# When the next piece of x is asked for: one transform slot earlier, from batch 2 on

## The chip, the cores and the metric

The kernel runs on one core of one Trainium2 chip. The metric is the device time of one execution in microseconds (us). Beside it one execution was profiled; every start time below counts from the start of that profile's span.

## What is computed

The reference mixes eight sequences with a Fourier transform and feeds the result to a mixture of experts (MoE). Cut to what matters:

```python
X = np.fft.rfft(x, axis=1)                  # x: 8 x 2496 x 256, float32
Yr = Xr @ w_r - Xi @ w_i + b_r
Yi = Xr @ w_i + Xi @ w_r + b_i
Yr, Yi = soft_threshold(Yr, 0.01), soft_threshold(Yi, 0.01)
x = np.fft.irfft(Yr + 1j * Yi, n=2496, axis=1)      # 19968 rows of 256
expert = argmax(x @ w_gate)                 # 8 experts
# per expert: the 80 rows of the largest gate value (softmax of x @ w_gate)
out[rows] = gate * (relu(x[rows] @ w1[e]) @ w2[e])  # all other rows are zero
```

## The kernel before

**Stages.** 2496 is 39 x 64, and the transform is done in two steps with a trip through HBM between them. Stage A (`stageA`, L283) multiplies a piece of x by a 39-point table, three blocks of 39 rows at a time on 117 partitions. Its result `zs`, split into a high and a low float16 half (`stageAz`, L303, on ACT and DVE), is stored to the HBM buffer `zd` (L319). `loadZ` (L329) reads it back turned round, stage B (L341) does the 64-point step, stage C (L394) the two weight products and the threshold, stage D (L485) turns the result and adds the gate columns, and stage HB (L524) does the first part of the way back and stores it to the HBM buffer `hd` (L539, L547). Once per batch stage E stores gate parts to `gd` (L675, L676) and reads them back as `gr` (L679) for a small product on TensorE (L723). After the eight batches the kernel chooses the rows, gathers them, runs the experts and scatters the rows into an output that `zfill` (L255, store at L259) has filled with zeros in 56 stores, most of 384 KB.

**The loop.** The main loop (L1346) has 16 steps, two per batch (`ch` 0 in an even step, 1 in an odd one). A step writes down the instructions of stages C and B, of D and HB for the step before, and three calls of `doA`, the transform slots: L1416, L1435 and L1448, here S1, S2 and S3. One slot transforms half a piece of x of a batch that comes two batches later. Steps 0 and 1 have more slots (8 and 4), so that batches 1 and 2 are done by the end of step 1; from step 2 on, batch b takes the six slots of one even and one odd step.

**Pieces.** A batch of x is three pieces, here (b,0), (b,1) and (b,2). `loadX` (L265) fetches one with three DMAs of 39 rows each on SP's queue: 3 x 312 KB for the first two, 234 + 234 + 156 KB for the third (39 rows x 8, 6 or 4 columns x 256 x 4 bytes). It goes into one of three buffers `xt`. A piece is transformed in two slots, a first and a second half. One slot ahead of its use a half is split into two float16 parts `xs` (`halve`, L275): a copy on ACT (L280), then a subtraction on GpSimd (L281), both of which wait for the piece's DMAs. There are two buffers `xs`.

**Who asks for the next piece.** `preX` (L1277) asks for pieces until two are waiting in the list `xls`, which by then doesn't hold the piece that is being transformed. `doA` (L1282) calls it when the second half of a piece has been written down (L1292). The piece asked for goes into the buffer of the piece before the present one. While `hold` is set (the last but one slot of step 0) `preX` does nothing.

**What orders SP's queue.** The instructions of an engine are issued in one fixed order, which a scheduler makes out of the order in which the program writes them down: an instruction that is ready sooner may be placed ahead of older ones, except that tiles of one name get their buffers in the written order. `pin` (`keep_in_program_order`, L161) ties an instruction behind the one that was written down just before it on the same engine. The loads of x (L270) and the zero stores (L259) are pinned; the stores to `zd` and `hd` and the loads of `z` are not. Stores are written down late: `flush` (L154) writes those that are pending, and it is called inside the stages.

Of the kernel before, what the change touches and what calls it, by code (L numbers as in the profile page):

```python
# [132 lines left out]
def fourier_mix_then_moe(ctx, tc, x, w_r, w_i, b_r, b_i, wg, w1, w2, t1, t2, vq, v3, v0, v1f, vt, sg, cst, cb, out):  # L133
# [131 lines left out]
    def loadX(b, c, xt=None):  # L265
        if xt is None:
            xt = zaq.tile([117, 8, 256], F32, name="xt", bufs=3)
        xv = x[b].rearrange("(a n) d -> a n d", n=64)
        for s, n in spans(c):
            pin(nc.sync.dma_start(xt[39 * s:39 * s + 39, :n], xv[:, 22 * s + 8 * c:22 * s + 8 * c + n]))  # L270
        return xt
# [3 lines left out]
    def halve(b, q, xt):  # L275
        j0 = 4 * (q % 2)
        ng = min(4, 22 - 4 * q)
        K = 117 if q < 5 else 78
        xs = halves[b, q] = zaq.tile([117, 2, 4, 256], F16, name="xs", bufs=2)
        nc.scalar.activation(xs[:K, 0, :ng], xt[:K, j0:j0 + ng], AF.Copy)  # L280
        nc.gpsimd.tensor_tensor(xs[:K, 1, :ng], xt[:K, j0:j0 + ng], xs[:K, 0, :ng], op=ALU.subtract)  # L281

    def stageA(b, q, xt):  # L283
        j0 = 4 * (q % 2)
        ng = min(4, 22 - 4 * q)
        K = 117 if q < 5 else 78
        xv = xt[:K, j0:j0 + ng]
        pt = psum()
        if b:
            if (b, q) not in halves:  # L290
                halve(b, q, xt)
            xs = halves.pop((b, q))
        for j in range(ng // 2):
            if b:
                for i, (t, h) in enumerate(((0, 0), (0, 1), (1, 0))):
                    nc.tensor.matmul(pt[:K, 512 * j:512 * j + 512], t1s[:K, t, :K], xs[:K, h, 2 * j:2 * j + 2], start=(i == 0), stop=(i == 2))  # L296
                continue
            nc.tensor.matmul(pt[:K, 512 * j:512 * j + 512], t1f[:K, :K], xv[:, 2 * j:2 * j + 2], start=True, stop=True)
        stageAz(b, q, K, ng, pt)
# [977 lines left out]
    def preX():  # L1277
        while len(xls) < 2 and Xq and not hold:
            a = Xq.pop(0)
            xls.append((a, loadX(*a)))  # L1280

    def doA(n=1):  # L1282
        for _ in range(n):
            if not Aq:
                if not xls:
                    preX()
                if xls:
                    (b, c), xt = xls.pop(0)
                    Aq.extend([(b, 2 * c, xt), (b, 2 * c + 1, xt)])
            if Aq:  # L1290
                stageA(*Aq.pop(0))
            if not Aq:  # L1292
                preX()
            if Aq:
                halve(*Aq[0])
            elif xls:
                (b, c), xt = xls[0]
                halve(b, 2 * c, xt)
# [47 lines left out]
    for i in range(len(steps)):  # L1346
        b, ch = steps[i]
# [66 lines left out]
        if i > 0:  # L1414
            zfill()
        doC(0, 0); doB(); doA(); doHB(); doB()  # L1416
        doP({12: 0, 13: 0, 14: 0}.get(i, 1)); doW({12: 1, 13: 1, 14: 1}.get(i, 1))
        if pend3:
# [11 lines left out]
        if i == 0:  # L1430
            doA(3)
        doP({12: 0, 13: 1, 14: 0}.get(i, 1)); doW({12: 1, 13: 1, 14: 1}.get(i, 1))
        if i > 0:
            zfill()
        doC(1, 0); doB(); doD(); doA(); doHB(); doD()  # L1435
        doP({12: 3, 13: 0, 14: 2}.get(i, 1)); doW({12: 1, 13: 1, 14: 1}.get(i, 1))
        if prev:
# [172 lines left out]
```

## Time and profile before

| | |
|---|---|
| time, median of 3 runs | 648.32 us (645.98 to 655.67) |
| the profiled execution's own time | 649.41 us |
| its span (first to last instruction) | 647.2 us, 2.2 us less |
| TensorE matmul (PE) busy | 543.1 us, 84% of the span |
| VectorE (DVE), GpSimd (POOL), ScalarE (ACT) busy | 426.5, 384.2, 335.2 us |
| moved by DMA | 133.17 MB, 206 GB/s on the mean |

PE is TensorE with its matmuls, PEld its weight loads. A name with q (SPq) is an engine's sequencer, which waits and issues DMAs. "Idle before" is the time that an engine sat idle just before an instruction, and "<-" names what ended it. Such a releaser is inferred: where an engine is named that had long been done, or a DMA of another buffer, the wait ended with a DMA that landed at that time. "DMA share" is the mean busy share of the core's 16 DMA engines; it can come out a little over 1.

### The profile page before, as it was taken

The page shows a single profiled execution, that of the slowest core. Times are in us where ns is not written, and L with a number is a line of the kernel's source. Part 1 is how long each engine was busy: PE and PEld are TensorE (multiplying, and loading weights), DVE is VectorE, ACT ScalarE, POOL GpSimd, SP SyncE. Part 2 cuts the span into 40 slices and gives each one's busy share as a digit, 9 for nine tenths or more (in the row PEclk, how much of TensorE's full clock was granted, in tenths as well). Part 3 has the DMA queues.
Part 4 walks back from the last instruction along what each step waited for, and adds up shares of the span by engine and source line. Part 5 has one row for each costly group of instructions (what it writes and reads, how often), then busy time and mean ns, then how long its engine had stood idle before and what let it go on. Part 6 is the DMA issues. An engine that isn't in the chain of part 4 may idle for free. (4 is left out here: it accounts for less than half of the span.)

```text
span 647.2 us, 12925 instructions
## 1 busy us (share of the span) xinstructions
PE 543.1 (84%) x5002; PEld 395.7 (61%) x5003; DVE 426.5 (66%) x768; ACT 335.2 (52%) x483; POOL 384.2 (59%) x292
## 2 busy tenths in 40 slices
PE   6349779999789998998999889988799895967783
PEld 2136447667666776685776557756577674436673
DVE  3424425476557665775776796689999977955870
ACT  1325546566546575574666545654656727411561
POOL 2014757676836775675768457667863458455671
PEclk7778979999999999998999989989899868888887
DMA  7797879689679968987997896699745368457630
GB/s 175 247 221 178 229 177 284 194 248 207 194 205 292 225 180 218 271 235 197 270 214 221 210 283 182 186 261 276 170 139 164 83 216 262 122 158 267 219 121 29
DMA packets 96456, 133.17 MB, mean 206 GB/s; under 512 B 27038, under 2 KB 78253, under 8 KB 94517
## 3 DMA queue, kind: packets, MB, share of 16 engines
q1 hardware_dynamic: 88885, 114.64, 67.0%
q0 software_dynamic: 2128, 9.25, 4.2%
q10 hardware_dynamic: 5376, 8.39, 4.1%
q8 instruction: 41, 0.67, 0.4%
q14 instruction: 26, 0.21, 0.1%
HBM read 69.58 MB, written 62.67 MB: 204 GB/s over the span
## 5 line engine op out<-in xcount | busy, mean ns | idle before, releaser
L406 PE MATMUL ps<-XT,WM 128*128 128x288 f16 (+1 forms) x1536 | 224.2, 304 | 15.0 <-ACT XT L355 6.0
L406 PEld LDWEIGHTS <-WM 128*128 128x128 f16 x1536 | 152.3, 100 | 77.2 <-issue 18.4
L281 POOL TENSOR_TENSOR xs<-xt,xs 117x1024 f16<-117x1024 f32 (+1 forms) x42 | 82.6, 1967 | 56.8 <-ACT xs L280 36.4
L446 POOL TENSOR_TENSOR YT<-R,YT 128x1408 f16<-128x1408 f32 (+1 forms) x28 | 73.4, 2620 | 49.9 <-ACT YT L445 49.9
L414 ACT ACTIVATE tp<-ps,thr 128x674 f32<-128x674 f32 (+1 forms) x64 | 49.8, 778 | 80.1 <-PE ps L406 75.3
L420 DVE SCALAR_TENSOR_TENSOR R<-ps,thr,tp 128x674 f32<-128x674 f32 (+1 forms) x56 | 48.4, 865 | 56.8 <-ACT tp L414 56.5
L350 PE MATMUL ps<-t2s,z 128*128 128x128 f16 (+1 forms) x320 | 59.8, 224 | 19.6 <-DMA z<-zd 17.2
L356 DVE TENSOR_TENSOR XT<-ps,XT 128x640 f16<-128x640 f32 (+2 forms) x64 | 52.0, 817 | 36.6 <-ACT XT L355 36.6
L313 DVE TENSOR_TENSOR zs<-ps,zs 117x1024 f16<-117x1024 f32 (+1 forms) x45 | 51.1, 1136 | 23.6 <-ACT zs L312 23.3
L296 PE MATMUL ps<-xs,t1s 117*117 117x512 f16 (+1 forms) x231 | 59.8, 392 | 4.8 <-ACT xs L280 2.9
L423 POOL TENSOR_TENSOR R<-R,sgs 128x576 f32<-128x576 f32 x28 | 36.5, 1303 | 44.2 <-DVE R L420 35.6
L280 ACT ACTIVATE xs<-xt 117x1024 f16<-117x1024 f32 (+1 forms) x42 | 41.2, 983 | 40.5 <-DMA xt<-in_x 33.8
L351 PE MATMUL ps<-t2s,z 128*128 128x128 f16 (+1 forms) x320 | 59.6, 223 | 0.0
L352 PE MATMUL ps<-t2s,z 128*128 128x128 f16 (+1 forms) x320 | 59.4, 223 | 0.0
L355 ACT ACTIVATE XT<-ps 128x640 f16<-128x640 f32 (+2 forms) x64 | 44.4, 699 | 17.0 <-PE ps L352 13.0
L312 ACT ACTIVATE zs<-ps 117x1024 f16<-117x1024 f32 (+1 forms) x45 | 42.9, 953 | 18.0 <-PE ps L296 11.2
L502 PE MATMUL ps<-wgi,YT 128*128 128x144 f16 (+1 forms) x302 | 44.3, 230 | 8.7 <-ACT sall L753 5.7
L556 PE MATMUL ps<-YO,vqs 128*128 128x512 f16 (+1 forms) x252 | 50.6, 343 | 0.0
L514 DVE TENSOR_TENSOR YO<-ps,YO 128x768 f16<-128x768 f32 (+1 forms) x50 | 45.3, 906 | 7.7 <-ACT YO L513 7.7
L350 PEld LDWEIGHTS <-z 128*128 128x128 f16 (+1 forms) x320 | 31.8, 99 | 24.8 <-DMA z<-zd 18.1
L445 ACT ACTIVATE YT<-R 128x1408 f16<-128x1408 f32 (+1 forms) x28 | 35.4, 1265 | 19.6 <-POOL R L442 19.4
L503 PE MATMUL ps<-wgi,YT 128*128 128x136 f16 (+1 forms) x302 | 44.0, 227 | 1.5 <-POOL YT L446 1.4
(281 smaller groups left out, 1024.7 us busy)
## 6 DMA issues: line engine op xcount, KB each, us to landing
out<-zero SPq DMA_DIRECT2D x48, 384.0 KB
hd<-hs SPq DMA_DIRECT2D x94, 192.0 KB
zd<-zs SPq DMA_DIRECT2D x114, 156.0 KB
xt<-in_x SPq DMA_DIRECT2D x48, 312.0 KB
z<-zd SPq DMA_DIRECT2D x16, 576.0 KB
wt<-in_moe_w ACTq DMA_DIRECT2D x10, 512.0 KB
z<-zd SPq DMA_DIRECT2D x7, 704.0 KB
z<-zd SPq DMA_DIRECT2D x7, 640.0 KB
```

The lines of the kernel that those rows point to most:

```text
L281: nc.gpsimd.tensor_tensor(xs[:K, 1, :ng], xt[:K, j0:j0 + ng], xs[:K, 0, :ng], op=ALU.subtract)
L296: nc.tensor.matmul(pt[:K, 512 * j:512 * j + 512], t1s[:K, t, :K], xs[:K, h, 2 * j:2 * j + 2], start=(i == 0), stop=(i == 2))
L313: nc.vector.tensor_tensor(zs[:K, :ng, 1, :], pv[:K, :ng], zs[:K, :ng, 0, :], op=ALU.subtract)
L350: nc.tensor.matmul(o, zz(0), t2s[:K, cl, 0, :], start=True, stop=False)
L351: nc.tensor.matmul(o, zz(0), t2s[:K, cl, 1, :], start=False, stop=False)
L352: nc.tensor.matmul(o, zz(1), t2s[:K, cl, 0, :], start=False, stop=True)
L356: nc.vector.tensor_tensor(ov(1), pv, ov(0), op=ALU.subtract)
L406: nc.tensor.matmul(pt[:, 512 * k:512 * k + n], WM[:, dh, m, wh, 128 * eh:128 * eh + 128], XT[:, dh, xh, c, c0 + n * k:c0 + n * k + n], sta ...
L414: nc.scalar.activation(fv(t), pv, AF.Relu, bias=thr[:, eh, ri, 0:1])
L420: nc.vector.scalar_tensor_tensor(fv(Rf), pv, thr[:, eh, ri, 1:2], fv(t), op0=ALU.add, op1=ALU.min)
L446: nc.gpsimd.tensor_tensor(yv(1), rv, yv(0), op=ALU.subtract)
L556: nc.tensor.matmul(o, tab[:, v], yo(h), start=(i == 0), stop=(i == 2))
```

## The change

In `doA`, when a piece is taken from the list to transform its first half, and its batch is 2 or higher, `preX` is called at once, ahead of the transform of that half. The call after the second half stays; it then finds two pieces waiting and does nothing.

```diff
                 if xls:
                     (b, c), xt = xls.pop(0)
                     Aq.extend([(b, 2 * c, xt), (b, 2 * c + 1, xt)])
+                    if b > 1:
+                        preX()
             if Aq:
                 stageA(*Aq.pop(0))
             if not Aq:
                 preX()
```

## Rows read from the trace of the kernel before

**Rows 1.** Busy time by stretch: five stretches of the main loop, each about one batch long. Columns: the stretch; its length; busy us of each engine with the number of instructions; the TensorE clock granted (1.00 is 2.4 GHz); DMA share; GB/s.

```profile
85.00:144.00 59.00, 52.24 (x446) 37.63 (x444) 30.52 (x40) 33.98 (x45) 40.84 (x30) 0.94 0.86 234
144.00:202.50 58.50, 51.75 (x477) 38.40 (x476) 34.47 (x53) 32.78 (x47) 37.29 (x30) 0.97 0.86 217
202.50:261.00 58.50, 55.69 (x515) 41.33 (x514) 40.26 (x60) 36.00 (x51) 39.44 (x31) 1.00 0.88 226
261.00:319.00 58.00, 55.30 (x501) 40.60 (x500) 37.74 (x57) 34.38 (x50) 38.69 (x31) 0.97 0.86 229
319.00:377.00 58.00, 53.79 (x502) 39.98 (x500) 43.18 (x80) 33.90 (x49) 38.45 (x31) 1.00 0.89 236
```

**Rows 2.** What PE waited for from 100 to 377 us, the three longest in total. Columns: us in total, times, longest.

```profile
PE ps L723 <- DMA gr<-gd: 7.4, 4, 3.4
PE ps L502 <- ACT sall L753: 5.7, 3, 2.5
PE ps L502 <- DVE R L420: 1.6, 1, 1.6
```

**Rows 3.** The page's group of ACT's copy that splits x, over the whole span. Behind the first bar its busy us and mean ns, behind the second the idle us before it and what ended most of that.

```profile
L280 ACT ACTIVATE xs<-xt 117x1024 f16<-117x1024 f32 (+1 forms) x42 | 41.2, 983 | 40.5 <-DMA xt<-in_x 33.8
```

**Rows 4.** The same copies in ACT's timeline, for seven halves. Columns: start us, us, engine and line, what, and in brackets the idle us before it.

```profile
129.05 1.06 ACT L280 ACTIVATE xs<-xt 117x1024 f16<-117x1024 f32 x1 [4.28 <-DMA xt<-in_x]
...
190.31 1.06 ACT L280 ACTIVATE xs<-xt 117x1024 f16<-117x1024 f32 x1 [4.91 <-DMA xt<-in_x]
...
248.91 1.06 ACT L280 ACTIVATE xs<-xt 117x1024 f16<-117x1024 f32 x1 [4.55 <-DMA hd<-hs]
...
267.88 1.06 ACT L280 ACTIVATE xs<-xt 117x1024 f16<-117x1024 f32 x1 [1.79 <-DMA xt<-in_x]
...
288.04 1.07 ACT L280 ACTIVATE xs<-xt 117x1024 f16<-117x1024 f32 x1
...
307.08 1.06 ACT L280 ACTIVATE xs<-xt 117x1024 f16<-117x1024 f32 x1 [2.14 <-DMA hd<-hs]
...
364.07 1.06 ACT L280 ACTIVATE xs<-xt 117x1024 f16<-117x1024 f32 x1 [3.35 <-DMA xt<-in_x]
```

**Rows 5.** PE's timeline, the matmuls ahead of which PE was idle within 7 us after one of those copies.

```profile
131.61 0.22 PE L350 MATMUL ps<-t2s,z 128*128 128x128 f16 x1 [1.13 <-DVE XT L356]
...
192.20 0.28 PE L502 MATMUL ps<-wgi,YT 128*128 128x144 f16 x1 [2.55 <-ACT sall L753]
...
250.80 0.22 PE L502 MATMUL ps<-wgi,YT 128*128 128x144 f16 x1 [2.18 <-ACT sall L753]
...
365.96 0.22 PE L502 MATMUL ps<-wgi,YT 128*128 128x144 f16 x1 [0.99 <-ACT sall L753]
...
370.05 0.22 PE L502 MATMUL ps<-wgi,YT 128*128 128x144 f16 x1 [1.56 <-DVE R L420]
```

**Rows 6.** SP's timeline from 233 to 287 us, with some rows left out. Columns: start us, us for the whole row, line, what, how many DMAs.

```profile
233.44 0.72 SPq L679 DMA_DIRECT2D gr<-gd  x2
234.21 2.58 SPq L259 DMA_DIRECT2D out<-zero  x3
236.88 3.36 SPq L319 DMA_DIRECT2D zd<-zs  x3
240.34 1.57 SPq L270 DMA_DIRECT2D xt<-in_x  x3
...
249.29 0.62 SPq L336 DMA_DIRECT2D z<-zd  x1
...
250.64 0.64 SPq L259 DMA_DIRECT2D out<-zero  x1
...
260.71 1.92 SPq L270 DMA_DIRECT2D xt<-in_x  x3
...
263.19 3.01 SPq L270 DMA_DIRECT2D xt<-in_x  x3
266.31 0.63 SPq L336 DMA_DIRECT2D z<-zd  x1
...
268.80 9.22 SPq L319 DMA_DIRECT2D zd<-zs  x6
280.05 4.20 SPq L547 DMA_DIRECT2D hd<-hs  x6
...
286.18 0.62 SPq L675 DMA_DIRECT2D gd<-gh  x1
```

**Rows 7.** Busy time by stretch as in rows 1, for the same batch; the last two columns are DMA share and GB/s.

```profile
236.00:248.00 12.00, 11.93 (x97) 8.29 (x96) 8.15 (x14) 4.56 (x6) 7.72 (x6) 1.00 0.87 234
248.00:252.00 4.00, 1.82 (x20) 1.26 (x18) 1.33 (x2) 2.83 (x5) 1.96 (x1) 1.00 0.56 139
252.00:288.00 36.00, 35.81 (x358) 27.43 (x357) 25.88 (x36) 23.07 (x32) 25.45 (x21) 1.00 1.00 273
288.00:296.00 8.00, 5.81 (x38) 3.86 (x37) 4.20 (x8) 4.50 (x8) 7.09 (x7) 0.91 0.48 102
```

**Rows 8.** PE's timeline, the first matmul of stage B that reads the `z` loaded at 249.29.

```profile
269.86 0.23 PE L350 MATMUL ps<-t2s,z 64*128 64x128 f16 x1
```

**Rows 9.** What SP waited for from 100 to 377 us, two rows. Columns as in rows 2.

```profile
SPq L319 <- DMA xt<-in_x: 14.6, 11, 2.5
SPq L679 <- DMA gd<-gh: 12.0, 4, 3.3
```

## The prediction

> **What bounds the kernel now.** I read the busy time by stretch first. In the main loop a batch takes 58 to 59 us, and PE is busy for 51.8 to 55.7 of them [rows 1]; the next, DVE and GpSimd, reach 43.2 and 40.8 at most. So the loop goes at PE's pace, and only what leaves PE idle can be won back: over the five stretches, 292 us long, the five PE sums make 268.8, which leaves 23 us. The second view is what PE waited for [rows 2]. The three longest entries from 100 to 377 us are the gate parts `gr` (7.4 us in 4 waits), `sall`, an ACT instruction (5.7 in 3), and a DVE instruction (1.6). No load of x is among them. Whoever stopped here would call the change worthless.
>
> The third view goes one engine back. ACT's copy of x sat idle for 40.5 us, of which 33.8 was put down to the load of x [rows 3]; in ACT's timeline these are waits of 1.8 to 4.9 us before the first half of a piece [rows 4]. (At 248.91 and 307.08 the view names an `hd` store; the copy reads nothing but x, so the DMA that let it go was a load of x.) ACT issues in order, so everything behind the copy stands too. PE's timeline right after it shows what that costs [rows 5]: 190.31 waited 4.91, and at 192.20 PE had been idle 2.55, waiting for `sall` on ACT; 248.91 waited 4.55, PE 2.18 at 250.80; 364.07 waited 3.35, PE 0.99 at 365.96; 129.05 waited 4.28, PE 1.13 at 131.61. The differences are 2.36, 2.37, 2.36 and 3.15. So PE has some 2.4 us of work in hand, and a wait shorter than that is free: 1.79 and 2.14 [rows 4] have no PE idle in rows 5. So the 5.7 us of `sall` are the x loads under another name.
>
> The fourth view is SP's queue [rows 6]. Batch 5 is the pattern: (5,1) is issued at 240.34 and lets ACT go at 248.91, 8.6 us later; (5,2) goes out at 260.71, (6,0) at 263.19. The waits of over 2.4 us are all for a (b,1): the pieces first split at 129.05, 190.31, 248.91 and 364.07.
>
> **What the change moves.** By the code, the call after the second half now finds two pieces waiting and adds nothing, so no DMA and no byte is added. The piece still goes into the buffer of the piece before the present one, whose last reader ran a slot earlier; for (5,1) that is the buffer of (4,1), some 30 us free, so no new wait for a buffer. While batch 2's first piece is taken, `hold` is set and the call does nothing; so the first piece that moves is (3,0), and 15 pieces with 45 DMAs move. Where each goes on SP follows from what was written down just before it, to which it is pinned.
>
> (b,1) was asked for in S3 of an odd step, behind the step's third zero store and stores to `zd`; now it is asked for in S2, ahead of both, and pinned to the second zero store. The three zero stores start at 234.21 and take 2.58, 0.86 each, so the load starts near 235.9 in place of 240.34: 4.4 us sooner. Counted in bytes, one zero store of 384 KB and three `zd` stores of 156 KB no longer go ahead of it, 0.87 MB, at 234 GB/s [rows 7] 3.7 us. Of the two I take the smaller. The waits of 4.91, 4.55, 4.28 and 3.35 shrink to 1.2 or less, under the 2.4 that PE has in hand. That wins PE's whole idle there: 2.55 + 2.18 + 1.13 + 0.99 = 6.85 us. At 370.05 another 1.56 stands 5 us behind the last of these waits; it may belong to it. The term lies between 0 (ACT is let go, PE isn't) and 8.4; I take 6.85, the sum of the rows right behind the waits.
>
> (b,2) was asked for in S2 of an even step; now in S1. The zero store to which it is pinned is issued early (such a store at the head of a step is the one at 250.64, ten us before the next one). What holds it is the rule that buffers go in written order, so it goes right behind (b,1): about 238 in place of 260.71. The wait for (5,2), 1.79 at 267.88 [rows 4], was under the 2.4: worth 0 to PE. But its 0.64 MB leaves a stretch in which the DMA engines were full (252 to 288, share 1.00) for one with room (236 to 248, share 0.87, and 0.56 after it) [rows 7]. If that lets the gate parts land sooner, up to 7.4 us of PE's idle for `gr` [rows 2] could go; if it changes nothing, 0. I take 0, since the third piece moves the other way.
>
> (b+1,0) was asked for in S1 of the odd step, pinned to the early zero store, and so was issued at 263.19. Now it is asked for in S3 of the even step, behind the first three of the six `zd` stores that start at 268.80. So one slot sooner in the program puts it later on the queue, near 272. With the 8.6 us that (5,1) took it lands near 281, and it is split at 288.04 without a wait [rows 4, 6]: 7 us of cover, cost 0. If the cover is gone, each us past 2.4 costs one, in each of four batches.
>
> What stands behind the moved loads: the `zd` and `hd` stores of that stretch and the load of `z` at 249.29. New ahead of it are (b,2)'s 0.64 MB, 2.7 us at 234 GB/s. The `z` is first read at 269.86 [rows 8], 20 us after its issue: cost 0. SP issues three DMAs more by then, 1.9 us as at 260.71, in a stretch in which it has waits of its own.
>
> Here a rule of the Trainium skill speaks against the change. In rows 6 and 7 a load that goes ahead takes its 0.64 to 0.96 MB of the DMA engines from what comes after. "DMA: Bandwidth & Descriptors", section "Queues, rings and completion order", says that each DMA engine consumes the descriptors of a ring in their order. By that rule every us that a moved load wins is lost by the transfers behind it; the sum stands as long as nobody waits for those, and the third rival is the case in which somebody does.
>
> The sum is -6.85 us: 649.41 becomes 642.56 for the profiled execution. That one is 1.1 us above the median of the three runs, 648.32; against the median it is 641.5, which I forecast.
>
> **Rivals.**
>
> The idle moves on. PE comes 2 us sooner to its next wait, `gr`, and waits that much longer there. For it: SP waits 12.0 us in 4 times for the gate parts to land between store and load [rows 9], and this doesn't get shorter. Against it: the chain of `gr` begins with PE's own work of the same step, which comes sooner too. Time: 648.3 to 646.
>
> The order doesn't follow. The scheduler may place the loads where they were, or place the copies on ACT so much earlier that ACT waits again. For it: (b+1,0) shows that a place in the program is not a place on the queue. Against it: (b,1) is pinned, and its new neighbour is known. Time: 648.3.
>
> Slower: (b+1,0) gets in front of the gate parts. At 272 its 0.96 MB stand ahead of the last three `zd` stores, six `hd` stores and the gate store at 286.18, in a stretch with a DMA share of 1.00. At the 273 GB/s of that stretch [rows 7] that is 3.5 us on the landing for which SP waits [rows 9], and PE stands at `gr` for as long, in four batches: 14 us, less the 6.85, makes +7.2 and 655.5. It decides from where the DMA engines stay full up to the gate store. SP's waits of `zd` stores for a landing x, 14.6 us in 11 [rows 9], would then grow as well. Against it: this load stood in the same stretch before, the 0.64 MB of (b,2) leave it, and right after 288 the share falls to 0.48.
>
> Faster than forecast: the relief reaches `gr`. With 1.56 and all of 7.4 it is 632.5, with half of the latter 636.
>
> **How the numbers follow.** Forecast 0.52, with its own range 640 to 645 (from 8.4 us won down to half of the term, 3.4); the idle moves on 0.20; the order doesn't follow 0.06; slower 0.14; faster than forecast 0.08. The range 635 to 654 takes in both no-change rivals, half of the slower one and half of the fastest. A change of 2% is about what a measurement of this kernel can tell from none: 635.4 and 661.3. Only the fastest case reaches the first, and the slower one reaches the second if the wait is twice as long: faster 0.07, same 0.87, slower 0.06.
>
> **What would show it.** Right: (b,1)'s loads start between two zero stores, 4 to 5 us sooner against the `gr` loads; (b,2) follows at once; the waits of ACT's copy fall from 33.8 us to about half (those of the pieces before (3,0) stay), and PE's entry for `sall` is gone. (b+1,0) stands among the six `zd` stores. Wrong: PE's entry for `gr` well over 7.4; ACT's copies of a (b,0) with waits over 2.4; the waits of ACT's copy gone and PE's idle per batch still over 3 us (the second would mean that the idle moved on); or the loop's stretch longer than 58 us with the DMA share at 1.00 up to the gate store.

## The result, and the profile after

The changed kernel took 632.26 us on the median against 650.84 for the kernel before in the same job; the ratio is 0.967 [0.956, 0.977]. Two repeats gave 0.980 [0.975, 0.985] and 0.971 [0.959, 0.983]. So it is 13 to 22 us faster, where 6.85 were forecast, and 632.26 lies below the range. The ratios leave out slow runs, which the medians have in them, and one of these, the execution profiled first, took 2672.65 us (the same kernel's others 625 to 633), so the rows of after come from a later profile of it (`e1_again`, 632.65 us on the median, span 630.8 us).

Only SP's order differs between the two kernels; PE, ACT and GpSimd get the same instructions in the same order, and on DVE one memset changes places with its neighbour. So the same stretch of work can be cut out of both: from the 289th matmul of L406 to the 1057th, some four batches. Columns as in [rows 1]; of the kernel after, this stretch last, two batches ahead of it:

```profile
160.00:215.00 55.00, 54.32 (x508) 40.51 (x507) 39.44 (x58) 34.79 (x50) 39.63 (x31) 1.00 0.85 235
215.00:269.50 54.50, 53.82 (x504) 40.13 (x502) 38.93 (x58) 34.29 (x50) 39.13 (x31) 1.00 0.90 249
...
145.55:367.50 221.95, 216.86 (x2018) 161.55 (x2016) 165.29 (x261) 137.55 (x196) 157.13 (x120) 1.00 0.88 243
```

The same stretch of the kernel before, in the profile behind the prediction:

```profile
146.79:388.43 241.64, 222.56 (x2019) 163.79 (x2017) 164.67 (x262) 140.44 (x197) 157.99 (x121) 0.98 0.88 228
```

And in a second profile of the kernel before (`b1_again` below, 643.08 us):

```profile
147.22:386.56 239.34, 224.35 (x2018) 164.27 (x2016) 162.86 (x261) 139.69 (x196) 156.56 (x121) 0.97 0.88 228
```

The stretch is 17.4 to 19.7 us shorter. PE's idle time in it (length less busy) fell from 19.1 and 15.0 to 5.1 us, and the busy time of the same matmuls fell from 222.6 and 224.4 to 216.9, with the granted clock at 1.00 where it was 0.98 and 0.97. In a second profile of the kernel after (`e5_change` below) the stretch takes 223.3 us, 218.2 of them busy, with the clock at half (1.2 GHz) for 3.4 us near its end. Of DMA nothing was saved: the share stays at 0.88.

What PE waited for from 100 to 377 us [rows 2], the four longest:

```profile
PE ps L406 <- DVE R L420: 3.6, 5, 2.6
PE ps L350 <- DVE zs L313: 3.5, 1, 3.5
PE ps L350 <- DVE R L420: 1.8, 1, 1.8
PE ps L406 <- DVE hs L563: 1.7, 4, 0.4
```

Both long entries of before are gone, `sall` (5.7) as forecast and `gr` (7.4) too. The second line is a single stall at 374 us, behind the stretch; more on it under `e5_change`. Not all of the gain in the stretch is kept: from its end to the end of the span the kernel after takes 263 us (259 in `e5_change`), the kernel before 259 and 254. ACT's copy [rows 3] waits 15.3 us in place of 33.8:

```profile
L280 ACT ACTIVATE xs<-xt 117x1024 f16<-117x1024 f32 (+1 forms) x42 | 41.2, 984 | 15.3 <-DMA xt<-in_x 15.3
```

In ACT's timeline [rows 4] the first halves of (5,1), (5,2), (6,0) and (6,1) come without a wait but for 0.63 us:

```profile
234.20 1.06 ACT L280 ACTIVATE xs<-xt 117x1024 f16<-117x1024 f32 x1
...
254.37 1.05 ACT L280 ACTIVATE xs<-xt 117x1024 f16<-117x1024 f32 x1
...
276.07 1.07 ACT L280 ACTIVATE xs<-xt 117x1024 f16<-117x1024 f32 x1
...
289.77 1.06 ACT L280 ACTIVATE xs<-xt 117x1024 f16<-117x1024 f32 x1 [0.63 <-DMA xt<-in_x]
```

SP's timeline of the same batch [rows 6]:

```profile
222.59 0.72 SPq L679 DMA_DIRECT2D gr<-gd  x2
...
224.33 2.77 SPq L270 DMA_DIRECT2D xt<-in_x  x3
227.14 0.36 SPq L259 DMA_DIRECT2D out<-zero  x1
227.60 1.55 SPq L270 DMA_DIRECT2D xt<-in_x  x3
...
251.34 1.04 SPq L336 DMA_DIRECT2D z<-zd  x1
...
254.94 2.02 SPq L319 DMA_DIRECT2D zd<-zs  x3
257.05 3.05 SPq L270 DMA_DIRECT2D xt<-in_x  x3
261.96 1.69 SPq L319 DMA_DIRECT2D zd<-zs  x3
263.97 6.19 SPq L547 DMA_DIRECT2D hd<-hs  x6
270.26 1.80 SPq L319 DMA_DIRECT2D zd<-zs  x3
272.17 0.62 SPq L675 DMA_DIRECT2D gd<-gh  x1
```

This is the queue that the prediction drew: (5,1) between two zero stores, (5,2) right behind, (6,0) among the six `zd` stores. From the first of the six to the gate store it takes 17.2 us where it took 17.4, so at first sight nothing is won there. But the gate store has to be measured against PE's own work.

**The gate store against PE.** The last matmul on the way to `gh` (L662) ended at 274.85 before, and the gate store left 11.33 us later; after, it is 263.23 and 8.94. The first part of that is `gh` itself. DVE's timeline before:

```profile
276.50 1.23 DVE L313 TENSOR_TENSOR zs<-ps,zs 117x1024 f16<-117x1024 f32 x1 [1.10 <-ACT zs L312]
...
279.70 0.33 DVE L674 SCALAR_TENSOR_TENSOR gh<-gdif 128x48 f32<-128x48 f32 x2
```

and after:

```profile
263.70 1.21 DVE L313 TENSOR_TENSOR zs<-ps,zs 117x1024 f16<-117x1024 f32 x1
...
266.43 0.33 DVE L674 SCALAR_TENSOR_TENSOR gh<-gdif 128x48 f32<-128x48 f32 x2
```

The first waited 1.10 us for ACT, which had waited 1.79 us for (5,2) at 267.88 [rows 4]; `gh` was complete 5.18 us behind L662, now 3.52. The second part is SP, 6.15 us behind `gh` before and 5.42 now.

**What holds SP.** In the traces the DMAs of SP (and those of ACT, in `g1_act` below) use eight semaphores in turn, and the program has a DMA wait for the landing of the one that had its semaphore, eight places earlier. Worked out for the second half of that row of the kernel before, from the semaphore events of its trace (times in us):

```
DMA issued at       the one eight earlier, issued   landed
zd store  271.94    x (6,0)     263.19              271.92
zd store  273.48    x (6,0)     264.38              273.42
zd store  275.47    x (6,0)     265.88              275.46
zd store  277.72    z load      266.31              277.71
hd store  280.05    z load      266.99              279.99
hd store  281.04    zero store  267.67              281.02
```

Each is issued within 0.1 us of that landing. The gate store's own place was free 1.1 us before it was issued; it is late because SP issues in order, and the stores ahead of it had waited. A load of (6,0) took some 9 us to land there, and the `z` loads and the zero store issued behind six loads of x took 11 to 13, and each held one place. In the kernel after the `z` loads and the zero store come ahead of (6,0), at 251.34 to 254.50, and land 8.4 to 9.5 us later.

### The profile page after: what moved, and what is told of

It reads as the page before. It is cut to its first block, busy times and chain, and to the rows that moved or that the text cites. A ratio compares the mean times of both kernels' runs of the same rounds, so it can differ in the third digit from the quotient of the medians.

```text
span 2670.8 us, 12926 instructions
## 1 busy us (share of the span) xinstructions
PE 2650.1 (99%) x5002; PEld 1348.6 (50%) x5003; DVE 416.0 (16%) x768; ACT 347.7 (13%) x483; POOL 382.5 (14%) x292
## 5 line engine op out<-in xcount | busy, mean ns | idle before, releaser
L406 PE MATMUL ps<-XT,WM 128*128 128x288 f16 (+1 forms) x1536 | 1197.0, 1139 | 0.0
L406 PEld LDWEIGHTS <-WM 128*128 128x128 f16 x1536 | 476.6, 311 | 663.9 <-issue 661.5
L296 PE MATMUL ps<-xs,t1s 117*117 117x512 f16 (+1 forms) x231 | 321.2, 1707 | 0.0
L556 PE MATMUL ps<-YO,vqs 128*128 128x512 f16 (+1 forms) x252 | 249.0, 1300 | 0.0
L350 PE MATMUL ps<-t2s,z 128*128 128x128 f16 (+1 forms) x320 | 215.2, 673 | 8.3 <-DMA z<-zd 8.3
L351 PE MATMUL ps<-t2s,z 128*128 128x128 f16 (+1 forms) x320 | 221.8, 693 | 0.0
L352 PE MATMUL ps<-t2s,z 128*128 128x128 f16 (+1 forms) x320 | 219.6, 686 | 0.0
L502 PE MATMUL ps<-wgi,YT 128*128 128x144 f16 (+1 forms) x302 | 198.2, 708 | 0.0
L503 PE MATMUL ps<-wgi,YT 128*128 128x136 f16 (+1 forms) x302 | 195.2, 691 | 0.0
L296 PEld LDWEIGHTS <-t1s 117*117 117x117 f16 (+1 forms) x231 | 107.5, 487 | 138.9 <-issue 136.5
L350 PEld LDWEIGHTS <-z 128*128 128x128 f16 (+1 forms) x320 | 94.0, 294 | 70.0 <-issue 46.2
L351 PEld LDWEIGHTS <-z 128*128 128x128 f16 (+1 forms) x320 | 94.7, 296 | 27.0 <-issue 18.0
L502 PEld LDWEIGHTS <-YT 128*128 128x128 f16 x302 | 90.6, 300 | 27.9 <-issue 11.2
L352 PEld LDWEIGHTS <-z 128*128 128x128 f16 (+1 forms) x320 | 99.1, 310 | 10.8
L503 PEld LDWEIGHTS <-YT 128*128 128x128 f16 x302 | 90.7, 301 | 26.4 <-issue 13.3
```

Of the source, the lines that this page charges most:

```text
L350: nc.tensor.matmul(o, zz(0), t2s[:K, cl, 0, :], start=True, stop=False)
L351: nc.tensor.matmul(o, zz(0), t2s[:K, cl, 1, :], start=False, stop=False)
L352: nc.tensor.matmul(o, zz(1), t2s[:K, cl, 0, :], start=False, stop=True)
L406: nc.tensor.matmul(pt[:, 512 * k:512 * k + n], WM[:, dh, m, wh, 128 * eh:128 * eh + 128], XT[:, dh, xh, c, c0 + n * k:c0 + n * k + n], sta ...
L502: nc.tensor.matmul(pt[:, off:off + w], yt(0), wgi[:, eh, 0:w], start=True, stop=False)
L503: nc.tensor.matmul(pt[:, off:off + w - w % 128 // 2], yt(1), wgi[:, eh, 0:w - w % 128 // 2], start=False, stop=True)
```

## The experiments

The kernel before ran beside each experiment (medians 646.85, 647.47 and 650.55 us in the three jobs). Collected from the traces, for the four batches of the loop that read `gr`: how long behind L662 `gh` is complete, and the gate store leaves; PE's idle for `gr` and the waits of ACT's copy from 100 to 377 us; and the ratio of times:

| kernel | `gh` behind L662, us | gate store behind L662, us | idle for `gr` | copy's waits | ratio |
|---|---|---|---|---|---|
| before | 6.1, 3.6, 5.2, 4.8 | 14.9, 10.3, 11.3, 11.3 | 7.4 | 28.2 | |
| b1_again (before) | 5.4, 4.9, 5.4, 4.8 | 12.3, 11.4, 12.3, 11.5 | 8.4 | 24.9 | |
| e1_again (change) | 3.5, 3.5, 3.5, 3.5 | 8.2, 8.9, 8.9, 9.2 | 0 | 3.5 | 0.980 |
| e5_change (change) | 3.5, 3.5, 3.5, 3.5 | 7.8, 8.6, 8.9, 8.0 | 0 | 0 | 0.971 |
| e2_b1 | 3.5, 6.5, 4.2, 3.5 | 10.7, 13.0, 11.6, 9.5 | 6.8 | 9.1 | 0.984 |
| e3_b2 | 3.5, 3.3, 3.5, 3.5 | 9.2, 8.9, 11.9, 9.4 | 2.6 | 16.1 | 0.989 |
| e4_b0 | 5.1, 5.2, 5.9, 5.6 | 10.6, 8.3, 9.7, 10.0 | 1.9 | 28.8 | 0.987 |
| p2_10 | 4.4, 6.5, 3.5, 3.5 | 9.4, 9.6, 8.0, 8.2 | 0 | 7.8 | 0.973 |
| p1_12 | 3.5, 3.5, 3.3, 3.5 | 8.6, 10.5, 11.8, 10.9 | 4.7 | 3.8 | 0.990 |
| z1_small | 5.4, 4.4, 4.0, 3.5 | 11.7, 9.3, 9.8, 8.5 | 2.4 | 14.3 | 0.985 |
| z2_small | 3.5, 3.5, 3.5, 3.5 | 5.8, 4.6, 4.2, 4.0 | 0 | 2.0 | 0.972 |

Where nothing stops PE it reaches L723 17.3 us behind L662 (in all eight batches of the two profiles of the change). A store up to some 9 us behind L662 is therefore free, and of what it is later PE waits the greater part: with the store at 10.7, 11.6 and 13.0 us PE came to L723 after 19.2, 19.8 and 21.4 (`e2_b1`).

### The change in one line, and its three parts

```diff
-                    Aq.extend([(b, 2 * c, xt), (b, 2 * c + 1, xt)])
+                    Aq.extend([(b, 2 * c, xt), (b, 2 * c + 1, xt)]); b > 1 and preX()             # e1_again
+                    Aq.extend([(b, 2 * c, xt), (b, 2 * c + 1, xt)]); b > 1 and c == 2 and preX()  # e2_b1: only (b,1) sooner
+                    Aq.extend([(b, 2 * c, xt), (b, 2 * c + 1, xt)]); b > 1 and c == 0 and preX()  # e3_b2: only (b,2) sooner
+                    Aq.extend([(b, 2 * c, xt), (b, 2 * c + 1, xt)]); b > 1 and c == 1 and preX()  # e4_b0: only (b+1,0) moved
```

> The changed kernel once more, written on one line so that line numbers agree with the kernel before, to get a profile of an ordinary execution. On PE, ACT and GpSimd its instructions stand in the order of the kernel before, on DVE one memset changes places with its neighbour; only SP's order differs. Both theories: 0.967 of the kernel before (0.956 to 0.977). Theory W (the waits of ACT's copy for (b,1) cost PE's idle behind them, 6.9 us, and the rest is something else): `sall` gone from PE's waits, and another PE wait of some 11 us in total gone or a later stretch shorter. Rival D (the full stretch of the DMA engines held SP and with it the gate parts): PE's wait for `gr` gone too, the DMA share of the stretch ahead of the gate store under 1.00.

> Only the requests for the second pieces (b,1) come a slot sooner; (b,2) and (b+1,0) are asked for where they were. Theory W: this alone carries the term of the prediction, -6.9 us, ratio 0.989, and the waits of 3.4 to 4.9 us of ACT's copy fall under 2.4. Rival D: -2 us or less, ratio 0.997 or more, since the full stretch stays.

> Only the requests for the third pieces (b,2) come a slot sooner, which puts them right behind (b,1). Theory W: nothing, ratio 1.00, since these waits were shorter than what PE has in hand. Rival D: the larger part, -8 to -12 us, ratio 0.982 to 0.988, with PE's wait for `gr` shorter.

> Only the requests for the first pieces (b+1,0) come a slot sooner, which puts them later on SP's queue, among the stores to `zd`. Theory W: nothing, ratio 1.00. Rival D: some of it, -3 us (0.995), since 0.96 MB come later in the full stretch; if these loads get in front of the gate parts instead, +3 to +14 us (1.005 to 1.02).

Measured: 632.65 (0.980 [0.975, 0.985]), 635.99 (0.984 [0.980, 0.989]), 638.68 (0.989 [0.984, 0.995]) and 639.63 (0.987 [0.983, 0.991]). Each part alone gains 7 to 10 us. Theory W had 6.9, 0 and 0 us for the three, rival D 2 or less, 8 to 12, and 3. So W failed on (b,2) (6.9 us [3.3, 10.5]) and (b+1,0), and D on (b,1) and (b+1,0). D's sign in the whole change, a DMA share under 1.00 ahead of the gate store, decides nothing: in the last 12 us ahead of it the share is 0.89 to 0.92, and in the kernel before 0.88 to 0.95. With (b,1) alone `sall` is gone from PE's waits and `gr` stays; the two longest from 100 to 377 us:

```profile
PE ps L723 <- DMA gr<-gd: 6.8, 3, 2.5
PE ps L406 <- DVE R L420: 3.9, 6, 2.6
```

In the traces (b,1) alone makes the stretch of four batches 3.9 to 6.2 us shorter (235.4 us); the rest of its 10.2 us lies behind the stretch, and no run here shows why.

With (b+1,0) alone it is the other way round:

```profile
PE ps L502 <- ACT sall L753: 3.6, 3, 1.5
PE ps L723 <- DMA gr<-gd: 1.9, 1, 1.9
```

So there are two gains, and the part that goes out later on the queue makes most of the second: `gh` is as late as before, but the gate store leaves 3 to 5.5 us behind it in place of 6 to 9. (b,2) alone gains in another way: ACT no longer waits for it, and `gh` is complete 3.5 us behind L662. The three parts add up to 4.0%, twice the whole in this job: (b,2) and (b+1,0) take away the same idle.

### The kernel before once more

> The kernel before, unchanged (a comment at the end of a line), for a second profile. Both theories expect the same SP queue and time (643 to 650). What is steady from execution to execution: PE's idle ahead of L502 behind the (b,1) copies 6 to 8.5 us in all, ahead of L723 6 to 9 us in all from 100 to 377 us; the granted clock at half for some 3.4 us behind each idle of PE over 2 us in the loop, and nowhere else in it. The last 60 us, where the four kernels run so far were 4 to 5 us shorter than the first profile, should be shorter here too if that belonged to the one execution.

It took 643.08 us. In PE's timeline, one wait for `gr` and two behind copies that waited 2.97 and 4.07 us:

```profile
175.54 0.63 PE L723 MATMUL ps<-gr,v1fs 78*78 78x256 f32 x2 [2.36 <-DMA gr<-gd]
...
190.68 0.22 PE L502 MATMUL ps<-wgi,YT 128*128 128x144 f16 x1 [0.61 <-ACT sall L753]
...
365.58 0.22 PE L502 MATMUL ps<-wgi,YT 128*128 128x144 f16 x1 [1.72 <-ACT sall L753]
```

The waits for `gr` are steady (8.4 us against 7.4). Those behind the copies aren't: the four places and the one at 370 make 4.6 us against the 8.4 of the prediction, fewer than expected. The work that PE has in hand is the same: 2.97 - 0.61 and 4.07 - 1.72 are 2.36 and 2.35, and at the place of 129.05 it is 3.15 us in both profiles. The last 60 us of the span were 4.5 us shorter here as well, so that difference belonged to the first profile. The clock was at half four times in the loop, 13.7 us in all, in the first profile three times, 10.2 us; one of the four:

```profile
176.80:180.20 3.40, 3.40 (x15) 1.87 (x13) 1.96 (x7) 1.11 (x2) 2.31 (x3) 0.50 0.86 245
```

Three of the four begin with or just after an idle of PE for `gr` of 1.85 to 2.36 us, the fourth behind 1.72 + 1.56 us at 365 to 370. Not every such idle is followed by one: after 3.40 us at 176.77 and 2.18 us at 250.80 in the first profile the clock stayed. So of the expectation "nowhere else" failed here, and "each idle" doesn't hold for the first profile.

### The gate store on another queue

```diff
-        nc.sync.dma_start(gd[b][0:21].rearrange("q n e -> n q e"), gh[0:64])
+        (nc.scalar if b < 6 else nc.sync).dma_start(gd[b][0:21].rearrange("q n e -> n q e"), gh[0:64])
```

(and so for L676; `g1_act` on the kernel before, `g2_act` on the change)

> The kernel before, but the two stores of the gate parts (L675, L676) go out on ACT's queue in place of SP's for batches 0 to 5; loads of x stay where they were. Theory Q (SP's queue, at most eight DMAs of SP in flight, held the gate store 6 to 9 us): the store leaves within 2 us of the last write of gh, PE's idle ahead of L723 falls from 7.4 us to under 2, the idle behind the (b,1) copies stays at some 7; 7 to 9 us less than before, ratio 0.986 to 0.989. Rival D (DMA engines full, not the queue): the store leaves sooner and lands as late, or SP gets to the load no sooner; idle ahead of L723 stays at 5 or more, ratio 0.996 to 1.00. A cost of its own: ACT waits for DVE's write of gh, up to 2 us per batch, which PE sees only beyond the 2.4 us it has in hand.

> The change, and the two gate stores on ACT's queue as in the run beside it. Theory Q: the idle ahead of L723 was gone already, so the stores' other queue adds nothing: within 2 us of the change alone (631 to 635, ratio 0.976 to 0.982), and the change on top of the ACT stores is worth only the waits of ACT's copy, some 7 us. Rival D: no interaction, the change is worth its 13 to 14 us here as it was alone, and the sum of both shows.

Measured: 666.94 us, ratio 1.027 [1.020, 1.035], and 640.68, 0.990 [0.984, 0.995]. Both expectations failed; both kernels got slower than without the edit, by some 19 us, and by some 8 against the change in the job before (632.65). ACT's timeline of `g1_act` tells why (ACTq is its sequencer):

```profile
159.18 0.18 ACT L671 ACTIVATE gh<-ps 64x24 f32<-64x24 f32 x1
167.06 0.65 ACTq L675 DMA_DIRECT2D gd<-gh  x1
167.75 1.40 ACTq L676 DMA_DIRECT2D gd<-gh  x1
169.19 0.74 ACT L414 ACTIVATE tp<-ps,thr 128x576 f32<-128x576 f32 x1 [9.83 <-issue]
```

`gh` was complete at 161.4, and the store left at 167.06 all the same, from a queue with nothing ahead of it. Its semaphore had last been used by an `hd` store that SP issued at 163.28 and that landed at 166.96. So leaving SP's queue doesn't free the gate store: the eight places, which all these DMAs share, hold it as well. On ACT the wait is worse, as ACT stands behind it and PE behind ACT:

```profile
170.84 0.88 PE L406 MATMUL ps<-XT,WM 128*128 128x288 f16 x3 [8.85 <-DVE R L420]
```

### Pairs of the parts

```diff
+                    Aq.extend([(b, 2 * c, xt), (b, 2 * c + 1, xt)]); b > 1 and c and preX()       # p2_10: (b,1) and (b+1,0)
+                    Aq.extend([(b, 2 * c, xt), (b, 2 * c + 1, xt)]); b > 1 and c != 1 and preX()  # p1_12: (b,1) and (b,2)
```

> The edit with the condition b > 1 and c: (b,1) early and (b+1,0) later on the queue as in the change, (b,2) left where it was before (ahead of the six zd stores). Theory Q: the (b,1) waits go (7 us) and the gate store goes out as early as with (b+1,0) alone (3.1 to 5.5 us after gh), so the idle at L723 goes too: the whole change without its (b,2) part, 632 to 635, ratio 0.977 to 0.983. Rival D (bytes of (b,2) in the full stretch count): as much as (b,1) alone or little more, 635 to 637, ratio 0.984 to 0.988.

> The edit with the condition b > 1 and c != 1: (b,1) and (b,2) early as in the change; (b+1,0) goes out some ten us earlier on the queue than before (ahead of the hd stores of the even step) in place of later, so no load of x stands near the six zd stores. Theory F: what counts is that the loads are out of the stretch ahead of the gate store, so the store leaves 3 to 5.5 us behind gh and PE's idle at L723 is under 1 us; 630 to 635, ratio 0.974 to 0.983. Rival L (being behind the zd stores is what helped): gate store 6 us or more behind gh, idle at L723 5 us or more, as with (b,1) alone; 635 to 638, ratio 0.982 to 0.988.

`p2_10`: 628.48 us, 0.973 [0.968, 0.978], as the first theory had it or a little better. The gains of (b,1) and (b+1,0) alone, 10.2 and 8.5 us, add up to 18.7; together they gave 17.8 (0.0275 x 647.47). Moving (b,2) as well adds nothing that can be measured (0.973 without it, 0.967 to 0.980 with it): the stretch of four batches is 2.4 to 3.8 us shorter with it, and behind the stretch `p2_10` takes 255 us in place of 259 to 263.

`p1_12`: 641.82 us, 0.990 [0.981, 0.998]: the rival was right (its signs nearly so: 4.7 us of idle for `gr`, the gate store 5.1 to 8.5 us behind `gh`). Here (6,0) goes out at 243.87, and the `z` loads that the change issues at 251.34 follow at 259.42:

```profile
243.87 2.34 SPq L270 DMA_DIRECT2D xt<-in_x  x3
...
259.42 1.12 SPq L336 DMA_DIRECT2D z<-zd  x1
...
269.73 4.51 SPq L547 DMA_DIRECT2D hd<-hs  x6
...
276.40 0.61 SPq L675 DMA_DIRECT2D gd<-gh  x1
```

The first `hd` stores now wait for a `z` load and a zero store to land (269.66, 270.42), and the gate store leaves 8.5 us behind `gh`. A load of x that goes out early enough to be no part of the crowded stretch still pushes the others into it. Against the change, from which it differs by (b+1,0) alone, the stretch of four batches is 5.0 to 6.4 us longer (228.3 us), for 4.7 us of idle for `gr`; the time behind the stretch (265 us) is longer than with the change as well (263 and 259), which the gate store doesn't explain. The rule of the Trainium skill weighed above ("DMA: Bandwidth & Descriptors", "Queues, rings and completion order") is that each DMA engine takes the descriptors of a ring in their order. The trace agrees with what the prediction made of it, that the transfers behind a moved load lose what it wins: here the `z` loads, which go out behind (6,0), are issued 6.7 us later against L662 than in the change. In the change it is (b+1,0) itself that comes after, 19 us before it is split.

### Fewer bytes, the same order

```diff
-            n = min(4, 26 - r)
+            n = 1 if 16 < len(zq) < 44 else min(4, 26 - r)
```

(`z1_small` on the kernel before, `z2_small` on the change)

> The kernel before, with 27 of its 56 zero stores (those of about batches 2 to 5 of the loop) writing 1 row of 256 per partition in place of 4 or 2: 7.2 MB less, so part of the output isn't zeroed; number and order of all DMAs and instructions as before. Theory F (the DMA engines are full, so the eight transfers in flight land late, and that holds both the x loads and the gate store): waits of ACT's copy under 2.4 us, gate store at most 5 us behind gh, idle ahead of L723 under 1.5 us in all; 10 to 15 us less than before, ratio 0.976 to 0.985. Rival N (number and order of SP's DMAs sets it, not bytes): gate store still 6 us or more behind gh, idle at L723 5 us or more, ratio 0.99 to 1.00.

> The change, with the same 27 zero stores made small. Theory F: there is nothing left to win by order, so within 3 us of the run beside it (the change is worth 0 to 3 us here against 13 to 15 alone), 630 to 634, ratio 0.974 to 0.982. Rival N: the change is worth its 13 us here too; if the small stores do win something, 620 to 625.

Measured: 636.41 us, 0.985 [0.976, 0.994], and 629.03, 0.972 [0.964, 0.979]. With 7.2 MB less and every DMA in its place the kernel before loses two thirds of its idle for `gr` (2.4 us left, where theory F had under 1.5, and the gate store is 4.9 to 6.3 us behind `gh`, where it had 5 at most). So bytes count in how late the eight land, and both theories are half right. But order still counts: the change is worth some 7 us on top, 4.5 of them in the stretch of four batches (227.8 against 223.3), more than the 0 to 3 expected. On the change the gate store leaves 4.0 to 5.8 us behind L662 in place of 8 to 9, and PE gains nothing: the stretch of four batches takes 223.3 us in `z2_small` and in `e5_change` alike. Of these PE is busy for 218: what is left to win there is 5 us.

### The change once more

(no edit)

> The change once more, unchanged. If the order alone sets it: ratio 0.975 to 0.985 again, no idle of PE over 1 us from 105 to 355 us, and again an idle of some 3.5 us ahead of L350 near 374 us with the clock at half right before, which the kernel without the (b,2) part didn't have. If that stall belonged to the one execution: absent, and the span some 4 us shorter.

634.28 us, 0.971 [0.959, 0.983]. No idle over 0.43 us from 105 to 355 us. The stall ahead of L350 is there again at 372.51, with 1.96 us, but the clock is full at it; at half it is from 358.9 on, for 3.4 us. `p1_12` has the stall too (3.25), `p2_10` and `z2_small` don't: it was seen only with (b,1) and (b,2) both early and full zero stores. What ends it is DVE's `zs`, and DVE's timeline of `e1_again` shows why that is late:

```profile
372.75 0.11 DVE L885 MEMSET tok<- 128x64 int32 x1 [5.06 <-DMA cid<-tok]
372.80 1.23 DVE L313 TENSOR_TENSOR zs<-ps,zs 117x1024 f16<-117x1024 f32 x1
```

DVE stood 5.06 us ahead of clearing the buffer `tok` (part of choosing the rows), until the store of its older contents (L863, issued at 366.65) had landed at 372.61, and `zs` stood behind it. In `e5_change` and `p1_12` DVE stood 4.7 and 6.0 us there, in `p2_10` and `z2_small` 2.7 and 0.9. So this is another store in the crowded queue, which the sum didn't have.

## Why the prediction was wrong

**The waits of ACT's copy: right.** `sall` left PE's waits, the copy's waits fell to under half, PE's 2.36 us in hand showed again. (b,1) moved 5.2 us up against the `gr` load (6.90 us behind it before, 1.74 after), forecast 4.4. The 1.56 us at 370, left out of the term, belonged to it: gone in `e2_b1` and `e1_again`, and there in `e3_b2` and `e4_b0`. The size came from one execution: these idles make 8.4 us in it and 4.6 in `b1_again`. (b,1) alone gave 10.2 us by the clock [7.3, 13.1], more than its part in the loop; that the term of 6.85 lies so near is partly luck.

**The order on SP's queue: right** for all three pieces.

**The step that failed: the term for `gr`, taken as 0.** Two sentences made it. "The wait for (5,2), 1.79 at 267.88, was under the 2.4: worth 0 to PE": PE didn't stop for it, but ACT's and DVE's next work moved back, and with it `gh`, by 0.1 to 2.6 us per batch. And "I take 0, since the third piece moves the other way": (b+1,0) went where it was said to (4.7 us later against the `gr` load) and its cover held (19 us from issue to split), but going behind three `zd` stores and the `z` loads is a gain of its own, as the gate store then leaves 3 to 5.5 us behind `gh` in place of 6 to 9; alone the move gave 8.5 us [5.8, 11.1]. Bytes ahead of the gate store were counted, by which a load among the `zd` stores is worse than one ahead of them; what each DMA waits for before it is issued was not. And the slack was worked out for `sall` (2.36 us) but not for `gr`. The store was 1 to 6 us too late (9 us free, 10.3 to 14.9 taken), so what is taken off `gh` or off SP's passage is for the greater part PE's. In the kernel after PE's idle for `gr`, 7.4 and 8.4 us before, is 0.

**The clock: left out.** Rows 1 showed 0.94 to 1.00 per batch. The same 2018 matmuls took 5.7 us less busy time than in the first profile and 7.5 less than in the second, for 10.2 and 13.7 us at half clock there and none here. That is 29 and 43% of the gain in the loop. (In `e5_change`, with 3.4 us at half, the busy time is 4.3 and 6.1 us less.)

**The sum.** 14.0 us of idle and 5.7 of busy time against the first profile; 9.9 and 7.5 against the second. The forecast had 6.85 and 0, and nothing for the time behind the loop. "Faster than forecast: the relief reaches `gr`", 632.5 us, is what happened; it had 0.08.

**The slower rival** named the right place and the wrong direction: SP's waits of `zd` stores for a landing x, which were to grow, are 16.0 and 15.2 us in the two profiles after and 14.6 [rows 9] and 16.1 before, and the gate store goes out sooner. "The idle moves on" fell with PE's entry for `gr`.

## What to carry to other kernels

A wait that the bounding engine doesn't feel where it happens can reach it half a batch later through a chain that starts on the waiting engine: measure each such chain against the bounding engine's own work, as was done here with L662, L675 and L723, before calling a wait free. Where a fixed number of transfers are in flight, ask of each DMA which earlier one must land before it is issued, and put a load with time to spare behind the stores that somebody waits for. When short idles of the bounding engine go, look at its clock too.

## What the runs showed of the hardware

- A DMA on ACT's queue, with its data ready and nothing ahead of it, waited 5.6 us for a store of SP's to land, with which it shared one of the eight semaphores (`g1_act`: data ready at 161.4, landing at 166.96, issue at 167.06).
- In a stretch with a DMA share of 1.00 a 312 KB load of x landed some 9 us after its issue, two `z` loads of 576 KB and a 384 KB zero store behind six loads of x 11 to 13 (kernel before, 263 to 281 us).
- Each us at half the TensorE clock (1.2 GHz) cost some 0.55 us of busy time in this loop (5.7 for 10.2, 7.5 for 13.7, each against `e1_again`; 1.4 for 3.4 between `e5_change` and `e1_again`).
